# Queries and keys cast and turned inside the DMA, with key blocks of 96: one change to a fused attention and Fourier kernel

## The chip, the cores and the metric

The kernel runs on one core of a Trainium2 chip. The metric is the device time of one execution in microseconds (us), on the slowest core; here there is only one. Each kernel was run several times on the same chip as the kernel it is compared with. A run counts as slow when it lies more than 1.5% above the fastest of the same kernel. Ratios below use fast runs alone; medians are over all runs.

The engines are named as the profile names them: PE multiplies matrices, PEld loads its weights (beside PE), DVE is the vector engine, ACT the scalar engine, POOL is GpSimd, SP issues most of the loads. L344 is line 344 of the kernel that the trace belongs to. The same instruction has another line number in each version.

## The reference, cut to what matters

Attention in chunks of 32 queries; each chunk sees 8 memory rows and the keys from 16 before it to 8 after it. The result goes through a Fourier transform over sequence and features, a normalisation and a two-layer MLP.

```python
batch, n_heads, seq, head_dim, n_mem = 4, 8, 768, 64, 8
chunk, left_ctx, right_ctx = 32, 16, 8
for c in range(seq // chunk):
    k_full = concat([mem_k, k[c_start - 16 : c_end + 8]])      # clipped at the ends
    v_full = concat([mem_v, v[c_start - 16 : c_end + 8]])
    a = softmax(q_c @ k_full.T / sqrt(head_dim))
    out[c] = a @ v_full
x = out as (batch, seq, 512)
u = x + real(fft(fft(x, axis=1), axis=2))
result = u + relu(norm(u) @ w_ch1) @ w_ch2                      # 512 -> 2048 -> 512
```

## The kernel before

A "pair" is two heads. There are 16 pairs, four per batch, and a pair has 12 blocks of 64 queries. A plan written in the kernel gives every engine a fixed order of work before anything runs: an engine that has to wait does not take up later work. The cuts below keep the way of the keys, queries and values of one pair. Batch 0 is cast on DVE, later batches on POOL.

```python
RB = 8; QP = S // RB          # 96 partitions, each with 8 consecutive sequence rows
KP = QP + 8; NB = KP // 8; BS = 96; NT = S // 64

def e_load_q(n):              # 2 KB runs, fp32
    nc.sync.dma_start(qf[n % NS], q[b, 2*pr:2*pr+2].rearrange("h (p j) d -> p h (j d)", j=RB))
# ... e_load_k alike
def e_load_v(n, hh):          # values: own rows and memory rows; the rest is copied
    ...
def e_overlap(n, hh):
    nc.gpsimd.tensor_copy(v1[96:128, 0:NT, 0:D + 1], v1[0:32, 1:NB, 0:D + 1])

def e_cast_q(n, eng):         # eng: DVE in batch 0, POOL later
    eng.tensor_copy(qb_of[n].rearrange(cp_b), qf[n % NS].rearrange(cp_q, j=RB))
def e_turn_q(n):              # 8 transposes on PE, then ACT puts the rows into their natural order
    for j in range(RB):
        nc.tensor.transpose(trq[:, j*QP:(j+1)*QP], qb[:, j]..., ident_b[0:QP, 0:QP])
def e_qT(n):
    nc.scalar.copy(qT.rearrange("p (a j) -> p a j", j=RB), trq.rearrange("p (j a) -> p a j", j=RB))
# ... e_turn_k, e_kT alike; kTb holds key blocks at a pitch of 96, read 128 wide

def e_scores(n, g):
    for t6 in range(6):
        for hh in range(2):
            nc.tensor.matmul(sc[:, hh, t6, :], kT[r0:r0 + 64, t * BS:t * BS + P],
                             qT[r0:r0 + 64, ts(t, 64)], start=True, stop=True, ...)
...
t_w1 = [add("POOL", 0.7, lambda dt=dt: nc.gpsimd.dma_start(       # MLP weights, after batch 0
    w1_sb[:, dt, :], moe_w_ch1[ts(dt, P), :]), [x_last], moved=3.5) for dt in range(NDT)]
```

The softmax here doesn't subtract the row's maximum and nothing guards it: scores larger than these inputs give would overflow.

## Time and profile before

| | before |
|---|---|
| three runs, us | 341.11, 345.05, 346.55 |
| span of the profiled run, us | 339.3, granted clock 0.969 |
| PE busy, us | 289.6 |
| DVE, ACT, POOL busy, us | 183.2, 168.9, 80.6 |
| PE idle in the first 100 us | 28.6 |
| score matmuls (384), busy us | 12.8 |

Two more readings of before are needed for the comparison. First, two stretches of 20 us each. The columns are the stretch, its length, then busy us (and instructions) of PE, PE weight load, DVE, ACT, POOL, then granted clock, DMA share and GB/s.

```profile
40.00:60.00 20.00, 10.41 (x158) 8.54 (x158) 18.85 (x35) 15.18 (x24) 14.90 (x13) 0.98 1.12 205
60.00:80.00 20.00, 17.06 (x215) 13.96 (x216) 15.26 (x36) 10.39 (x18) 4.77 (x5) 0.85 1.14 196
```

PE works for 27 of these 40 us. (The DMA share sums the times of all packets over the 16 engines; it passes 1 where the recorded times of packets overlap.)

### The profile page before, as it was taken

How to read it: one execution, taken by the hardware profiler on the slowest of the kernel's cores; microseconds unless marked ns; L12 is line 12 of the kernel's file. 1: busy time of each engine (PE TensorE's matmuls, PEld its weight loads, DVE VectorE, ACT ScalarE, POOL GpSimd, SP SyncE). 2: the span in 40 equal slices, each digit the busy share in tenths (PEclk: the TensorE clock that was granted, in tenths of full speed). 3: DMA queues.
4: the chain of work that ended last, by engine and by line, in shares of the span. 5: the costliest groups of instructions: out<-in, count | busy, mean ns of one | idle time of the engine just before them, and what ended most of it. 6: DMA issues, size and time to landing. Idle time of an engine off the chain costs nothing.

```text
span 339.3 us, 6789 instructions
## 1 busy us (share of the span) xinstructions
PE 289.6 (85%) x2761; PEld 185.4 (55%) x2761; DVE 183.2 (54%) x356; ACT 168.9 (50%) x297; POOL 80.6 (24%) x89
## 2 busy tenths in 40 slices
PE   0678647969998886969999997898999999999995
PEld 0467536847565565547755654574445454554542
DVE  6964498868089899599773469782010100101001
ACT  7554885557637448676633623335436053250620
POOL 5634594224342637252001200000010000000000
PEclk9999999879999999898999999599999999999999
DMA  7999999999407785692063100000340100201001
GB/s 157 214 183 162 168 229 203 220 173 178 72 3 152 131 182 136 183 201 36 0 110 101 31 3 2 31 31 33 68 119 2 62 31 2 93 0 64 31 32 63
DMA packets 51839, 33.02 MB, mean 97 GB/s; under 512 B 40032, under 2 KB 42080, under 8 KB 51808
## 3 DMA queue, kind: packets, MB, share of 16 engines
q1 hardware_dynamic: 45376, 22.03, 36.9%
q0 software_dynamic: 2688, 4.19, 6.7%
q10 hardware_dynamic: 3744, 6.36, 4.9%
q8 instruction: 22, 0.36, 0.5%
q14 instruction: 9, 0.07, 0.1%
HBM read 28.11 MB, written 6.29 MB: 101 GB/s over the span
## 4 chain that ended last, share of the span: by engine, by line
PE 62%; DVE 14%; DMA 9%; ACT 4%; POOL 3%; issue 3%; SPq 3%; ACTq 0%; POOLq 0%
PE ph L496 23%; PE pc L510 22%; DMA qf<-in_q_dram 8%; PE xa L349 7%; PE pm L445 4%; PE ps L413 2%; SPq L261 2%; DVE zy L373 2%; DVE lo L403 2%; PE sc L325 1%; DVE ff L390 1%; DVE st L457 1%; DVE pq L381 1%; ACT e L333 1%; DVE pq L380 1%
## 5 line engine op out<-in xcount | busy, mean ns | idle before, releaser
L503 ACT ACTIVATE hT<-ph 128x384 f16<-128x384 f32 x128 | 61.2, 492 | 70.5 <-PE ph L496 70.3
L496 PE MATMUL ph<-unT,w_sb 128*128 128x384 f16 x512 | 92.2, 327 | 2.4 <-ACT hT L503 1.8
L510 PE MATMUL pc<-w_sb,hT 128*128 128x512 f16 x384 | 87.3, 382 | 0.0
L516 DVE SCALAR_TENSOR_TENSOR osb<-pc,rstd,xsb 128x512 f32<-128x512 f32 x24 | 17.8, 746 | 98.3 <-PE pc L510 98.3
L496 PEld LDWEIGHTS <-w_sb 128*128 128x128 f16 x512 | 48.3, 97 | 37.9 <-issue 8.2
L510 PEld LDWEIGHTS <-hT 128*128 128x128 f16 x384 | 37.2, 98 | 42.4 <-issue 1.5
L282 POOL COPY va<-va 32x780 f32<-32x780 f32 x32 | 36.2, 1138 | 50.0 <-DMA va<-in_v_dram 37.9
L333 ACT ACTIVATE e<-sc,mbias 128x384 f32<-128x384 f32 x64 | 33.7, 579 | 20.0 <-PE sc L325 19.1
L349 PE MATMUL xa<-va,e 128*64 128x65 f32 x768 | 35.4, 253 | 8.6 <-ACT e L333 3.7
L349 PEld LDWEIGHTS xa<-va,e 128*64 128x64 f32 x768 | 30.6, 162 | 15.7 <-issue 7.7
L463 ACT ACTIVATE un<-xsb,mu_s 128x512 f16<-128x512 f32 x24 | 17.3, 722 | 24.5 <-DVE mu_s L458 15.8
L359 DVE RECIPROCAL zs<-xa 128x6 f32<-128x6 f32 x32 | 6.1, 190 | 34.5 <-PE xa L349 34.3
L325 PE MATMUL sc<-qT,kTb 64*128 64x64 bf16 x384 | 12.8, 207 | 12.6 <-ACT kTb L314 11.0
L484 POOL TENSOR_SCALAR rstd<-mu_s 128x6 f32<-128x6 f32 x4 | 1.0, 244 | 89.7 <-DVE osb L516 83.7
L413 PE MATMUL ps<-cosS,lo 128*128 128x193 f16 (+1 forms) x72 | 16.6, 285 | 4.6 <-DVE lo L403 4.5
L274 POOL CAST qb<-qf 96x1024 bf16<-96x1024 f32 x12 | 14.9, 1242 | 20.8 <-DMA qf<-in_q_dram 11.9
L413 PE MATMUL ps<-cosS,hi 128*128 128x193 f16 (+1 forms) x72 | 16.7, 285 | 3.4 <-DVE ff L390 3.2
L425 ACT CAST up<-ps 128x386 f16<-128x386 f32 x16 | 9.7, 605 | 19.4 <-PE ps L413 17.8
L325 PEld LDWEIGHTS <-kTb 64*128 64x128 bf16 x384 | 8.8, 104 | 18.5 <-ACT kTb L314 12.3
L360 DVE TENSOR_TENSOR xsb<-xa,zs 128x384 f32<-128x384 f32 x32 | 17.8, 557 | 1.1
L398 ACT CAST hi<-ff 128x768 f16<-128x768 f32 x16 | 13.2, 832 | 10.1 <-DVE ff L390 9.9
L403 DVE TENSOR_TENSOR lo<-ff,hi 128x768 f16<-128x768 f32 x16 | 16.8, 1063 | 2.2 <-ACT hi L398 2.1
(90 smaller groups left out, 356.2 us busy)
## 6 DMA issues: line engine op xcount, KB each, us to landing
qf<-in_q_dram SPq DMA_DIRECT2D x16, 384.0 KB
kf<-in_k_dram SPq DMA_DIRECT2D x16, 384.0 KB
out_dram<-osb ACTq DMA_DIRECT2D x24, 256.0 KB, 2.0
va<-in_v_dram SPq DMA_DIRECT2D x32, 144.0 KB, 5.8
w_sb<-in_moe_w_ch_dram POOLq DMA_DIRECT2D x8, 512.0 KB, 16.1
va<-in_v_dram SPq DMA_DIRECT2D x32, 48.0 KB, 6.8
va<-in_mem_v_dram SPq DMA_DIRECT2D x32, 24.0 KB
unT<-un SPq DMA_TRANSPOSE x18, 2.4
```

Of the source, the lines that this page charges most:

```text
L282: nc.gpsimd.tensor_copy(v1[96:128, 0:NT, 0:D + 1], v1[0:32, 1:NB, 0:D + 1])
L325: nc.tensor.matmul(sc[:, hh, t6, :], kT[r0:r0 + 64, t * BS:t * BS + P], qT[r0:r0 + 64, ts(t, 64)], start=True, stop=True, tile_position=(r ...
L333: nc.scalar.activation(e1[:, :, :, ts(half, 32)], sc[:, :, 0:6, ts(half, 32)], AFT.Exp, bias=mbias[:, half:half + 1], scale=1.0 / math.sqr ...
L349: nc.tensor.matmul(xa[64 * half:64 * half + 64, st, hh, 0:65], e1[:, hh, t6, :], v1[:, 6 * g + t6, 0:65], start=True, stop=True)
L360: nc.vector.tensor_tensor(xs[b][:, 3 * g:3 * g + 3, 2 * pr * D:(2 * pr + 2) * D] .rearrange("p s (h d) -> p s h d", h=2), xa[:, :, :, 0:D] ...
L403: nc.vector.tensor_tensor(lo[:, ab].rearrange(fl), ff_of[b, par][:, ab].rearrange(fl), hi[:, ab].rearrange(fl), ALU.subtract)
L413: nc.tensor.matmul(out_[:, sp, :], part[:, ab, sp * 3 + st, c0:c1], tab[:, sp, st, :], start=(st == 0 and i == 0), stop=(st == 2 and i == 1))
L463: nc.scalar.activation(un, xs[b][:, kt, :], AFT.Identity, bias=mu_of[b][:, kt, 0:1], scale=-1.0)
L496: nc.tensor.matmul(ph[:, 0:384], w1_sb[:, dt, ts(ht, P)], unT_of[b][:, dt, sh * 384:(sh + 1) * 384], start=(dt == 0), stop=(dt == NDT - 1))
L503: nc.scalar.activation(hT_of[b, sh][:, ht, :], ph_of.pop((b, sh, ht))[:, 0:384], AFT.Relu, bias=0.0, scale=-1.0)
L510: nc.tensor.matmul(pc_of[b, sh, stl], hT_of[b, sh][:, ht, ts(stl, P)], w2_sb[:, ht, :], start=(ht == 0), stop=(ht == NHT - 1))
L516: nc.vector.scalar_tensor_tensor(osb, pc_of.pop((b, sh, stl)), rstd_of[b][:, st:st + 1], xs[b][:, st, :], ALU.mult, ALU.add)
```

## The change

Its intent: key blocks become exactly the 96 rows that a block of 64 queries can see (8 memory, 16 left, 64 own, 8 right), filled by DMA alone, so that POOL copies nothing. From batch 1 on, queries and keys are cast to bf16 by the DMA and turned by DMA transposes. PE, POOL and ACT are then rid of casts, transposes and copies. The core of the diff:

```diff
+OWN = NMEM + LEFT
+WIN = OWN + 64 + RIGHT                                   # 96
-    va = [spool.tile([P, NB, 66], FP32, ...) for i in range(6)]
+    va = [spool.tile([WIN, 2, NT, 66], FP32, ...) for i in range(3)]
-    kTb = [spool.tile([P, NB * BS], BF16, ...) ...]
+    kTb = [spool.tile([P, NT, WIN], BF16, ...) ...]
...
+    def e_load_qk(n, i):                                  # batches 1 to 3: fp32 to bf16 on the way
+        for hh in range(2):
+            nc.gpsimd.dma_start(dst[n % NS][0:QP, :, hh, :],
+                                src[b, 2 * pr + hh].rearrange("(p j) d -> p j d", j=RB))
+    def e_flip_q(n):
+        qT_of[n] = qT = apool.tile([P, RB, QP], BF16, tag="qT", bufs=2, name="qT")
+        nc.sync.dma_start_transpose(qT, qb[n % NS].rearrange("p j h d -> p (j h d)"))
+    def e_flip_k(n):
+        nc.sync.dma_start_transpose(kU[n % NKU][:, :, KR:KR + QP], kb[n % NS][0:QP]...)
...
-    def e_overlap(n, hh):                                 # and the clears, casts, PE turns of batches 1-3
-        nc.gpsimd.tensor_copy(v1[96:128, 0:NT, 0:D + 1], v1[0:32, 1:NB, 0:D + 1])
...
     def e_kT(n):
         nc.scalar.copy(
+            strided(kTb[n % NKT], NMEM, [[WIN, NT], [RB, 11], [1, RB]]),
+            strided(tr_of.pop((n, 1)), 0, [[64 // RB, NT], [1, 11], [KP, RB]])
+            if n < HP else
+            strided(kU[n % NKU], KR - KOFF, [[64 // RB, NT], [1, 11], [KS, RB]]))
     def e_scores(n, g):
-                nc.tensor.matmul(sc[:, hh, t6, :], kT[r0:r0 + 64, t * BS:t * BS + P],
-                                 qT[r0:r0 + 64, ts(t, 64)], ...
+                nc.tensor.matmul(sc[0:WIN, hh, t6, :], kT[r0:r0 + 64, t, :],
+                                 strided(qT[r0:r0 + 64], t * 64 // RB, [[1, 64 // RB], [QP, RB]]), ...
...
+            lq, lk = [add("POOL", 1.6, lambda i=i: e_load_qk(n, i),
+                          [t_cast[HP - 1]], take=(("qb", "kb")[i],), moved=1.8) for i in range(2)]
+            eq = add("SP", 0.1, lambda: e_flip_q(n), [lq, t_eq[0]], take=("qT",), ...)
+            tk = add("SP", 0.1, lambda: e_flip_k(n), [lk, t_uz[n % NKU]], take=("kU",), ...)
```

The turned queries lie as 8 groups of 96, so that 64 consecutive queries are read with a step of 96 elements. And `[t_cast[HP - 1]]`, by which the casts are to come after batch 0's last cast, is a condition in the plan's model.

## The prediction

> **What bounds the kernel now.** I read the page's slices first, then the chain that ended last in order of time, then four stretches of engine busy time, then the DMA view in narrow windows.
>
> From the page, busy tenths in 40 slices of 8.5 us:
>
> ```profile
> PE   0678647969998886969999997898999999999995
> ...
> DVE  6964498868089899599773469782010100101001
> ...
> POOL 5634594224342637252001200000010000000000
> ...
> DMA  7999999999407785692063100000340100201001
> ```
>
> The first ten slices are filled by DMA, not by PE; from slice 24 on PE is full and all else is nearly idle. The cuts below are mine: end of batch 0's attention (33 us), end of batch 1's (95), end of the last attention group (199), from the chain. Columns: stretch, its length, then busy us (and instructions) of PE, PE weight load, DVE, ACT, POOL, then granted clock, DMA share, GB/s.
>
> ```profile
> 0.00:33.00 33.00, 18.05 (x277) 15.20 (x279) 22.93 (x70) 19.64 (x28) 16.10 (x26) 1.00 1.07 181
> 33.00:95.00 62.00, 48.34 (x642) 36.77 (x638) 40.80 (x85) 40.74 (x68) 30.65 (x31) 0.94 0.99 172
> 95.00:199.00 104.00, 92.34 (x1135) 62.72 (x1132) 79.48 (x137) 59.80 (x107) 32.29 (x32) 0.97 0.51 104
> 199.00:340.00 141.00, 130.89 (x720) 70.69 (x718) 39.97 (x65) 48.74 (x95) 1.59 (x2) 0.97 0.12 40
> ```
>
> PE idles 14.9, 13.7 and 11.7 us in the first three, 40 us before the last attention ends. The DMA share is 1.0 for 95 us, then a half. The chain says what those 95 us wait for:
>
> ```profile
> 32.79 7.19 DMA qf<-in_q_dram
> ...
> 48.45 7.04 SPq L261
> ...
> 57.05 14.37 DMA qf<-in_q_dram
> 71.54 1.04 POOL qb L274
> ```
>
> So up to 72 us the input transfers carry the chain, with a POOL cast behind them. After 199 us there are only the MLPs and one Fourier stage, in PE's fixed order, ending at 339. **Two clocks** run: T, when the last attention group is through, and 140 us behind it.
>
> **What the Trainium skill says.** "DMA: Bandwidth & Descriptors", Specifications, asks for at least 512 B per transfer for line rate. The trace agrees. Two windows of 1 us, one of values (256 B runs), one of queries and keys (2 KB runs):
>
> ```profile
> DMA packets 527, 0.13 MB, mean 127 GB/s; under 512 B 527, under 2 KB 527, under 8 KB 527
> ...
> q1 hardware_dynamic: 527, 0.13, 142.2%
> ```
> ```profile
> DMA packets 113, 0.22 MB, mean 221 GB/s; under 512 B 5, under 2 KB 5, under 8 KB 113
> ```
>
> The same page, "SWDGE vs HWDGE vs iDMA": a cast during DMA can only be issued by GpSimd, the plain transpose only by the other queues. The change is built so; the casting queue here is the one of the weights. "SBUF — State Buffer" says that a VectorE operation with two SBUF inputs and a GpSimd operation that reads SBUF block each other. The trace agrees: POOL's value copy takes 827 to 4297 ns, and the DVE fold pq takes 1.27 us at 97 us, 0.83 at 209 when POOL is still. "TensorE: Matmul & The Clock Gate", Weight-path perf modes: fast weight load needs 128 weights not in fp32. Key blocks of 96 columns lose that in the score matmuls; no weight load of that kind is in this trace.
>
> **The change, part by part.** A pair is two heads; there are 16, four per batch.
>
> *PE.* Batches 1 to 3 lose 12 x 16 transposes. A group of 8 takes 0.37 to 0.39 us on the warm clock in the chain, so 24 x 0.38 = 9.1 us go, all from before T. The order of the changed kernel also moves MLP work: behind the last attention group stand 80 first-layer blocks and 65 second-layer blocks of four matmuls, against 81 and 72. With 0.65 and 0.86 us per block the tail sheds 0.65 + 6.0 = 6.7 us, which PE does before T instead. Score matmuls stay 384; their moving operand now steps 96 elements and the weights are 96 columns. A group of 12 takes 0.45 us; I allow 0.2 us more, 32 x 0.2 = 6.4 us, a guess. The value matmuls keep their column counts, hence their time.
>
> *POOL.* 32 value copies (36.2 us), 24 casts (14.9 + 13.0 us) and three large clears leave: 64 of its 81 busy us. It gets 48 casting DMAs to issue (a weight DMA takes 0.62 to 0.80 us of POOL, so an estimate of 40 us in sum, with nothing else to do). Copies stood between a landed value and its matmul, 0.83 us at least.
>
> *ACT.* 12 query copies (0.80 us) go, seven clears at the start too (4.3 + 2.1 us). The key copy grows from 832 to 1056 columns. ACT was at half load: worth little except in the first 10 us.
>
> *DVE.* Same work, but no POOL copies beside it. The 16 double pq and ff folds average 1.09 and 0.94 us against 0.85 undisturbed: 16 x (0.24 + 0.09) = 5 us, on the chain in the Fourier stages only; I count 3.
>
> *DMA.* Packets are counted by runs (the weights' queue shows it: 512 + 2048 runs + 8 x 16 completions = its 2688 packets). Before, a pair is 1728 value packets and 384 of 2 KB: 1728/527 + 384/113 = 3.3 + 3.4 = 6.7 us of all engines. Ten pairs and the weights (6.7% of the span, 23 us) make 90 us, and the DMA row goes quiet at 88: the sum holds.
> After, values are 2256 packets, since left, right and memory rows are fetched twice. A cast of q and k makes 4 x 768 = 3072 runs of 256 B read and 128 B written. Two transposes move 768 packets each; the transposes of this trace (2128 packets, 63.1% of 6 us) cost 28.5 ns of an engine, so 768 x 28.5/16 = 1.4 us each. How fast small packets go is the question. Saturated they came at 527 per us; the last two value loads alone took 18.6 ns each (1808 packets, 30.1% of 7 us), 860 per us. With the first rate a later pair costs 4.3 + 5.8 + 2.7 = 12.8 us, with the second 2.6 + 3.6 + 2.7 = 8.9 us. **I take 10.8**, against 6.7.
>
> **Sum.** T if DMA sets it: batch 0 until 33 us as now (four pairs at 4.3 + 3.4 = 31, plus the start), then 12 x 10.8 = 130, weights 23, twelve flips of the normalised rows at 0.95 us = 11, outputs and latencies 6: T = 203. T if PE's order sets it with its present idle: 198.9 - 9.1 + 6.7 = 196.5, less 3 (DVE), plus up to 6.4 (scores): 194 to 200. So the DMA bound lies slightly ahead. The tail is 140.4 - 6.7 = 133.7. 203 + 133.7 = 337 us of span, 2 to 3 below before. Where the rate is nearer 860 the span is 328 to 334. Before's runs lie 2 to 6 us above the profiled span; measured like the 345.05 median, and with the better rate somewhat likelier since neither POOL copies nor 2 KB queues stand in between, I say **336 us**.
>
> **Rivals.** (1) *PE bound with hidden transfers.* The DMA share of 0.51 from 95 to 199 us speaks for spare room, and POOL can issue loads far ahead; then transposes, copies and DVE blocking are saved and idle falls as well: span 322 to 330. Against it: three buffers per kind limit the lead. (2) *DMA becomes the bound.* Per pair it doubles at the slow rate; read-modify-write on 128 B could make casts slower than 256 B copies. At 12.8 us per pair T = 227 and the time is about 362. For it: 95 us already saturated. Against: MLP(0) is moved ahead of the waiting attention in PE's order, so there is filler. (3) *A head-of-line wait on SP.* Transposes wait for casts and stand in the same in-order queue as value loads; a late cast then delays later values too. It adds 5 to 15 us. (4) *Scores slow PE* by more than my 0.2 us per group: twice the present 0.45 us would add 14 us.
>
> **Range and chances.** 321 (rival 1, some idle gone) to 360 (rival 2). The faster line is near 338, just above my number, so faster over 2%: 0.48; within 2%: 0.28; slower: 0.24.
>
> **What would show it.** Casting queue: some 37,000 more packets, and their cost per packet (18 to 30 ns of an engine supports me; 45 refutes). PE transposes of the first batch alone. Score groups of 0.45 to 0.65 us. The end of the last value matmul near 200 us, and 134 us behind it. POOL busy under 25 us without issues. pq folds of 0.85 to 0.95 us. I am wrong if PE waits for qT, kTb or va grow past 15 us in the middle, or if score groups take 0.9 us.

## More of the kernel before

Second, the groups by line and form: line, engine, operation, output and inputs, shapes, count, then busy us and mean ns, and last the idle time before the group with what ended it.

```profile
L314 ACT COPY kTb<-trk 128x832 bf16<-128x832 bf16 x16 | 13.7, 854 | 5.6 <-PE trk L304 4.6 <-POOL va L282 0.9
...
L325 PE MATMUL sc<-qT,kTb 64*128 64x64 bf16 x384 | 12.8, 207 | 12.6 <-ACT kTb L314 11.0 <-ACT e L333 1.5
```

The copy of the turned keys into their blocks takes 854 ns on ACT, and the score matmuls read weights of 128 key columns.

## The result, and the profile after

The changed kernel takes 361.03 us (median of four, 358.30 to 361.70), the kernel before, measured with it, 344.03 (median of four, 341.11 to 346.55). The ratio is 1.051, with a 95% interval of 1.041 to 1.061. A ratio here is the mean time of one kernel's fast runs over the mean of the other's fast runs in the same rounds, so it is not quite the ratio of the medians. The change makes the kernel slower by 5%. The prediction of 336 us was wrong in direction, and the result lies just outside the range.

The spans agree with the times: 339.3 before, 356.6 after. The granted clock is no part of it (0.969 before, 0.979 after). The page of after, in tenths of 40 slices of 8.9 us, then its DMA queues with packets, MB and the share of the 16 engines' span:

```profile
PE   0672740057998999999968999989999999999995
...
DVE  7922334048880227888476885497740010201001
...
POOL 4071700330032422313300001000001000000000
...
DMA  4999999999309989969997242010160010100101
...
q1 hardware_dynamic: 68032, 19.48, 34.8%
q0 software_dynamic: 40320, 8.92, 29.4%
```

PE has a hole in slices 7 and 8 (about 53 to 71 us) that the kernel before does not have. PE's busy total hardly differs (290.6 against 289.6 us), and neither does DVE's or ACT's for the worse. So the time is waiting, and early. In numbers, by my own cuts: up to 100 us PE idles 53.3 us instead of 28.6. The last attention group ends at 229.5 us instead of 198.9, so that clock is 30.6 us late: PE idles 19.9 us more up to there (60.2 against 40.3) and works 10.7 us more. The part behind it takes 127.1 us instead of 140.4, 13.3 us less. The difference, 17.3 us, is that of the spans.

The same two stretches as before, now of after:

```profile
40.00:60.00 20.00, 7.57 (x117) 6.37 (x114) 9.19 (x25) 8.67 (x14) 2.98 (x4) 1.00 1.24 176
60.00:80.00 20.00, 5.06 (x60) 4.37 (x61) 3.50 (x4) 8.61 (x9) 5.97 (x8) 1.00 1.49 177
```

PE works 12.6 of the 40 us, and no other engine is busy for half of them, but the DMA share stays above 1. The chain that ended last, in order of time (start, us, what), names what is awaited:

```profile
49.56 4.39 SPq L281
...
54.06 15.35 DMA kU<-kb
...
69.49 6.86 DMA kU<-kb
...
76.43 0.88 ACT kTb L331
```

L281 is the transpose of pair 4's queries, `kU<-kb` that of pair 4's keys and then of pair 5's. From 50 to 76 us the chain is nothing but DMA transposes of the first two pairs of batch 1. The prediction had 1.4 us for each; here they take 15.4 and 6.9 us from issue to landing. The waits show how that reaches PE (us in all, times, longest us):

```profile
PE sc L344 <- ACT kTb L331: 21.5, 2, 20.3
DVE lo L422 <- ACT hi L417: 21.4, 6, 14.3
```

ACT stands before the key copy until the transpose has landed. Being in order, it holds the Fourier cast `hi` behind it, hence DVE, and PE stands before pair 4's scores with everything that comes later in its order.

The busy times of two groups have changed too:

```profile
L344 PE MATMUL sc<-qT,kTb 64*96 64x64 bf16 x384 | 27.3, 286 | 22.8 <-ACT kTb L331 21.5 <-ACT e L352 1.1 <-DMA qT<-qb 0.2
...
L331 ACT COPY kTb<-kU 128x1056 bf16<-128x1056 bf16 x12 | 24.1, 2028 | 19.1 <-DMA kU<-kb 17.9 <-DVE osb L535 1.2
...
L331 ACT COPY kTb<-trk 128x1056 bf16<-128x1056 bf16 x4 | 4.1, 1036 | 2.9 <-PE trk L321 2.9
```

The score matmuls cost 14.5 us more PE time than before, and one key copy of the later batches takes 2.03 us instead of 0.85. The last line is the same copy in batch 0, of the same size: it reads the turned keys from PSUM, in steps of 100 elements, and takes 1.04 us.

### The profile page after: what moved, and what is told of

Read it like the earlier page. It is cut to its first block, busy times and chain, and to the rows that moved or that the text cites. A ratio compares the mean times of both kernels' runs of the same rounds, so it can differ in the third digit from the quotient of the medians.

```text
span 356.6 us, 6371 instructions
## 1 busy us (share of the span) xinstructions
PE 290.6 (82%) x2569; PEld 183.8 (52%) x2569; DVE 171.8 (48%) x344; ACT 168.0 (47%) x278; POOL 52.7 (15%) x89
## 3 DMA queue, kind: packets, MB, share of 16 engines
q1 hardware_dynamic: 68032, 19.48, 34.8%
q0 software_dynamic: 40320, 8.92, 29.4%
## 4 chain that ended last, share of the span: by engine, by line
PE 66%; DVE 13%; DMA 11%; ACT 4%; SPq 3%; issue 2%; POOL 0%; ACTq 0%
PE pc L529 22%; PE ph L515 20%; PE xa L368 7%; DMA kU<-kb 6%; PE ps L432 6%; PE sc L344 5%; PE pm L464 5%; DMA lead<-in_k_dram 3%; DVE ff L409 2%; DMA va<-in_v_dram 2%; ACT e L352 2%; DVE zy L392 2%; SPq L293 1%; DVE lo L422 1%; SPq L281 1%
## 5 line engine op out<-in xcount | busy, mean ns | idle before, releaser
L515 PEld LDWEIGHTS <-w_sb 128*128 128x128 f16 x512 | 48.8, 97 | 41.5 <-issue 12.1
L352 ACT ACTIVATE e<-sc,mbias 96x384 f32<-96x384 f32 x64 | 33.4, 571 | 34.0 <-PE sc L344 25.8
L344 PE MATMUL sc<-qT,kTb 64*96 64x64 bf16 x384 | 27.3, 286 | 22.8 <-ACT kTb L331 21.5
L368 PE MATMUL xa<-va,e 96*64 96x65 f32 x768 | 35.9, 255 | 9.3 <-ACT e L352 6.5
L368 PEld LDWEIGHTS xa<-va,e 96*64 96x64 f32 x768 | 31.1, 165 | 18.9 <-issue 9.8
L344 PEld LDWEIGHTS <-kTb 64*96 64x96 bf16 x384 | 19.7, 145 | 28.6 <-ACT kTb L331 21.9
L331 ACT COPY kTb<-kU 128x1056 bf16<-128x1056 bf16 x12 | 24.1, 2028 | 19.1 <-DMA kU<-kb 17.9
L276 POOL DMA_DIRECT2D qb<-in_q_dram x24 | 18.8, 787 | 54.0 <-DMA qT<-qb 35.1
L482 ACT ACTIVATE un<-xsb,mu_s 128x512 f16<-128x512 f32 x24 | 17.3, 720 | 15.0 <-DVE mu_s L477 11.4
L276 POOL DMA_DIRECT2D kb<-in_k_dram x24 | 18.7, 781 | 35.7 <-DMA kU<-kb 34.4
L379 DVE TENSOR_TENSOR xsb<-xa,zs 128x384 f32<-128x384 f32 x32 | 17.8, 557 | 1.1
L470 DVE TENSOR_TENSOR xsb<-pm,xsb 128x512 f32<-128x512 f32 x24 | 16.1, 672 | 3.8 <-PE pm L464 3.6
L476 DVE BATCH_NORM_STATS2 st<-xsb 128x6 f32<-128x512 f32 x24 | 16.7, 694 | 0.8
## 6 DMA issues: line engine op xcount, KB each, us to landing
w_sb<-in_moe_w_ch_dram POOLq DMA_DIRECT2D x8, 512.0 KB, 17.4
```

Of the source, the lines that this page charges most:

```text
L276: nc.gpsimd.dma_start(dst[n % NS][0:QP, :, hh, :], src[b, 2 * pr + hh].rearrange("(p j) d -> p j d", j=RB))
L331: nc.scalar.copy(strided(kTb[n % NKT], NMEM, [[WIN, NT], [RB, 11], [1, RB]]), strided(tr_of.pop((n, 1)), 0, [[64 // RB, NT], [1, 11], [KP, ...
L344: nc.tensor.matmul(sc[0:WIN, hh, t6, :], kT[r0:r0 + 64, t, :], strided(qT[r0:r0 + 64], t * 64 // RB, [[1, 64 // RB], [QP, RB]]), start=Tru ...
L352: nc.scalar.activation(e1[:, :, :, ts(half, 32)], sc[0:WIN, :, 0:6, ts(half, 32)], AFT.Exp, bias=mbias[0:WIN, half:half + 1], scale=1.0 / ...
L368: nc.tensor.matmul(xa[64 * half:64 * half + 64, st, hh, 0:65], e1[:, hh, t6, :], v1[:, hh, 6 * g + t6, 0:65], start=True, stop=True)
L515: nc.tensor.matmul(ph[:, 0:384], w1_sb[:, dt, ts(ht, P)], unT_of[b][:, dt, sh * 384:(sh + 1) * 384], start=(dt == 0), stop=(dt == NDT - 1))
```

## The two theories

**Theory A, order and packets.** The eight weight loads (4.2 MB as written, not needed yet) are issued by POOL from 37 to 45 us, just ahead of pair 4's transposes. SP's view of the DMA queue shows the two transposes being issued (start, us):

```profile
45.30 8.65 SPq L281 DMA_TRANSPOSE qT<-qb  x1
54.06 5.62 SPq L284 DMA_TRANSPOSE kU<-kb  x1
```

The Trainium skill, "DMA: Bandwidth & Descriptors", Queues, rings and completion order, says that each DMA engine "round-robins between the queue rows it has work for, at *packet* granularity". If that holds here, the transposes, in packets of 256 B, move at the packet rate of the weights, however small they are. Three windows of 1 us of after (packets, MB, share). At 44 us, first-layer weights of 4 KB written per packet on q0:

```profile
q0 software_dynamic: 49, 0.19, 96.0%
q1 hardware_dynamic: 48, 0.01, 9.5%
```

At 62 us, second-layer weights of 1 KB per packet on q0:

```profile
q0 software_dynamic: 163, 0.15, 90.7%
q1 hardware_dynamic: 161, 0.04, 30.4%
```

At 69 us, as the weights end:

```profile
q1 hardware_dynamic: 683, 0.17, 102.7%
q0 software_dynamic: 122, 0.04, 36.0%
```

One packet of one queue for one of the other, at both sizes. (At 44 us the packets of q1 are still values; at 47 us, with the query transpose issued, the counts are 51 and 51.) When the other queue empties, q1 goes from 161 to 683 a microsecond. Theory A says: hold the weights back until the first two transposes have landed, and most of the loss goes.

**Theory B, a stepped operand.** The moving operand of the score matmuls steps by 96 bf16 elements, the source of the key copy by 128. The Trainium skill, "SBUF — State Buffer", in its note on cachelines, says that SBUF has 16-byte lines, that an access which goes to a new line pays, and that 8 bf16 elements lie within one. The traces of before and after agree in direction (12.8 and 27.3 us), but the number of weight columns changed with the step. Theory B says: make these rows contiguous, and score groups and key copies become short again. The rival within it: it is the 96-column weights that cost.

**Rivals to both.** The early casts delay batch 0 (the load of pair 3's keys is waited for 9.82 us in the chain); the new values by DMA, with rows fetched more than once, cost more than the copies they save; or the sheer number of packets is the bound, as the prediction's second rival had it. Each has a run below.

## The experiments

Medians of the kernel before in the three calls were 341.62, 342.87 and 342.22 us. Ratios are to it, in brackets the 95% interval. after was not measured again: its row is from its own call, in which the kernel before had 344.03.

| run | median us | ratio to before |
|---|---|---|
| after | 361.03 | 1.051 (1.041 to 1.061) |
| gate_casts | 361.01 | 1.057 (1.047 to 1.067) |
| gate_w | 341.35 | 1.001 (0.991 to 1.010) |
| gate_both | 339.86 | 0.998 (0.989 to 1.007) |
| natural | 351.33 | 1.032 (1.023 to 1.040) |
| wide | 359.38 | 1.055 (1.045 to 1.065) |
| blocks_only | 343.12 | 1.008 (0.997 to 1.019) |
| gates_natural | 332.18 | 0.973 (0.957 to 0.988) |
| all4 | 333.62 | 0.979 (0.971 to 0.988) |
| small_w | 365.48 | 1.075 (1.065 to 1.084) |
| before_gate | 342.84 | 1.010 (1.002 to 1.017) |
| natural_gate_w | 333.56 | 0.984 (0.977 to 0.992) |
| gates_natural_2 | 331.44 | 0.975 (0.967 to 0.983) |

So a difference to after depends on how it is taken. For gate_w it is 19.7 us by medians, 17 by ratios (5.0% of 342) and 14.6 by the spans of the profiled runs (356.6 and 342.0); for natural 9.7, 7 and 6.3. Where the text below gives one number, it is that of the medians.

### gate_w: the weights behind the transposes

From the changed kernel. A tiny POOL copy that reads pair 5's turned keys stands ahead of the first weight load. It is a real wait, on the landing of the transpose.

```diff
+    gate = cpool.tile([P, 2], BF16, name="gate")
+    def e_w1(dt):
+        if dt == 0:
+            nc.gpsimd.tensor_copy(gate[:, 1:2], kU[(HP + 1) % NKU][:, 0, KR:KR + 1])
+        nc.gpsimd.dma_start(w1_sb[:, dt, :], moe_w_ch1[ts(dt, P), :])
```

> The changed kernel with one small POOL copy ahead of the first weight load; it reads pair 5's turned keys, so that no weight load starts before the transposes of pairs 4 and 5 have landed. Order theory (on an engine a 256 B packet of a transpose takes turns with a 4 KB packet of the weights, 50 small packets per us instead of 700 or more): pair 4's key transpose lands at 55 us instead of 69, the 20.3 us wait of the score matmuls for kTb falls to 4 to 8, time 346 to 352. Volume theory: the weights come later, the first MLP matmuls wait for them instead, about 360.

Measured: 341.35 us, 15 to 20 us less than after and below the 346 expected. One line removes the loss against before. The transposes, from SP's view, and the second of the two stretches:

```profile
42.19 1.57 SPq L282 DMA_TRANSPOSE qT<-qb  x1
43.88 1.38 SPq L285 DMA_TRANSPOSE kU<-kb  x1
...
56.91 11.51 SPq L285 DMA_TRANSPOSE kU<-kb  x1
```

```profile
60.00:80.00 20.00, 17.13 (x174) 14.16 (x176) 13.05 (x26) 9.77 (x15) 3.88 (x5) 0.83 1.24 163
```

The query transpose is issued in 1.57 us instead of 8.65, the key transpose in 1.38 instead of 5.62. Pair 4's key copy starts at 54.9 us instead of 69.5, and PE is busy 17.1 of 20 us where it was 5.1. The weights are now issued from 54.2 to 59.3 us, 17 us later than in after, yet the MLP's first matmul comes at 87.0 us instead of 101.5: nothing on PE waits for weights in either trace. The slow issue has not gone: the third line is pair 6's key transpose, now beside the weights, over 11.51 us, but PE's wait for keys is down to 7.0 us in all. The order is shown as the cause. The packet counts above speak for turns by packet; the next run was to test that against bytes.

### small_w: the same weight bytes in smaller packets

From the changed kernel, without a gate. Each first-layer load is split by columns, so that its packets are read in 2 KB runs and written in 1 KB runs, four times as many.

```diff
+    def e_w1(dt):
+        for c in range(4):
+            nc.gpsimd.dma_start(w1_sb[:, dt, ts(c, DFF // 4)],
+                                moe_w_ch1[ts(dt, P), ts(c, DFF // 4)])
```

> The changed kernel, no gate; the first MLP weight matrix is loaded in 16 casting DMAs of 512 columns instead of 4 of 2048, so the same bytes go in packets of a quarter of the size (2048 of 2 KB read and 1 KB written, instead of 512). Turn-taking theory (an engine gives each queue one packet in turn, so the small packets beside the weights go at the weights' packet rate): pair 4's transposes, which got 50 packets per us beside the large packets, get about 150 as they do beside the second matrix; its keys land near 57 us instead of 69, the score matmuls' wait for kTb falls from 20 us to 6 to 10, time 348 to 354. Bytes theory (the transposes stand behind the bytes of the weights): they land at 69 as before, 359 to 362.

Measured: 365.48 us, some 4 us slower than after (8 by ratios). The chain of small_w:

```profile
47.36 14.13 DMA kU<-kb
...
66.94 15.91 DMA kU<-kb
```

The first part came as expected: pair 4's key copy starts at 61.6 us, 8 us earlier than in after, and PE's longest wait for it is 10 us instead of 20. In a window of 1 us at 47 us the weights' queue has 180 packets and the other 131, where beside the large packets they had 49 and 48. But the expectation for the time was a miss. The weights now run beside pair 5's transposes as well (168 and 137 packets at 69 us), which land at 82.9 us instead of 76.4, and that wait of 15.9 us gives everything back. Nor is the test clean: POOL issues the 16 loads from 39.3 to 56.2 us, as it waits for earlier ones in between, where after issues its 4 from 37.2 to 39.7. So fewer weight bytes lay ahead of pair 4's transposes, and their earlier landing fits the bytes theory too. The turns rest on the packet counts. What the run does show is that smaller packets alone do not put the transposes first; the gate does.

### gate_casts and gate_both: the early casts

In after, POOL issues the casts of pairs 4 and 5 from 17.8 to 26.0 us, while batch 0's loads are still coming. The gate makes POOL wait for DVE's cast of pair 3, as the plan had meant.

```diff
     def e_load_qk(n, i):
+        if n == HP and i == 0:
+            nc.gpsimd.tensor_copy(gate[0:QP, 0:1], kb[(HP - 1) % NS][0:QP, 0, 0, 0:1])
```

> The changed kernel with one small POOL copy ahead of the first casting load; it reads what VectorE casts for pair 3, so that no casting load starts before batch 0's own fp32 loads have landed (in the changed kernel the casting loads of pairs 4 and 5 are issued at 17.75 to 26 us, and pair 3's keys land only at 33.8). Order theory (small packets of later pairs share the engines with the loads that are needed now): the last value group of batch 0 starts near 41 us instead of 49.6, PE's wait before pair 4's scores may grow as its casts start later; in all 3 to 8 us less, about 354. Volume theory (all of it must pass the engines anyway): 360, within 1 per cent.

Measured: 361.01 us, as after; the 3 to 8 us expected did not come. The early part is won, though half of it: batch 0's eighth value group starts at 45.2 us instead of 49.6 (41 expected), and pair 4's key copy at 50.7 instead of 69.5. It is lost again at once, as the chain of this run shows:

```profile
44.91 13.73 DMA w_sb<-in_moe_w_ch_dram
...
58.73 16.22 DMA kU<-kb
```

Pair 5's transpose now stands beside the weights and lands at 75 us, as in after. The gain upstream of this untouched wait was worth nothing.

With both gates:

> Both gates, the same bytes and packets as the changed kernel. Order theory: the PE idle time in the first 100 us goes from 53 us back to about 33 (29 in the kernel before), time 340 to 347. Volume theory: 356 to 361, since nothing is taken off the engines.

Measured: 339.86 us, 1.5 us less than gate_w alone, with overlapping runs (338.33 to 342.11 against 340.22 to 343.69). Pair 5's key copy starts at 56.0 us, 20 us earlier than in after, and PE idles 35.0 us in the first 100 (33 expected). The early casts are a cause of the second order.

### natural: contiguous rows after the transpose

From the changed kernel. Only the mapping of sequence rows to partitions in the casting load is exchanged. Partition p gets rows p, p+96, p+192, ... instead of 8 consecutive ones. The casting loads write 64 elements per run in either case. After the transpose the rows are in natural order.

```diff
-                                src[b, 2 * pr + hh].rearrange("(p j) d -> p j d", j=RB))
+                                src[b, 2 * pr + hh].rearrange("(j p) d -> p j d", j=RB))
...
-                 strided(qT[r0:r0 + 64], t * 64 // RB, [[1, 64 // RB], [QP, RB]]), ...
+                 qT[r0:r0 + 64, ts(t, 64)], ...
...      # key copy of the later batches
-            strided(kU[n % NKU], KR - KOFF, [[64 // RB, NT], [1, 11], [KS, RB]]))
+            strided(kU[n % NKU], 0, [[64, NT], [1, WIN - NMEM]]))
```

> The changed kernel, queries and keys of batches 1 to 3 loaded with 96 consecutive rows over the partitions (same runs of 64 elements, same packets), so that the turned queries and keys lie in natural order: the moving operand of the scores has step 1, the key copy reads runs. Stride theory: a score group of 12 falls from 0.77 us to 0.45 to 0.5, key copies from 2.03 us to 1.1, PE work before the last attention group falls by 24 or more groups x 0.3 = 8 us, time 350 to 354. Weight-load theory (96 columns lose the fast load): the group stays at 0.7 or more, time 357 to 360.

Measured: 351.33 us, 6 to 10 us less than after. The groups of natural:

```profile
L347 PE MATMUL sc<-qT,kTb 64*96 64x64 bf16 x384 | 17.6, 233 | 25.3 <-ACT kTb L337 20.2 <-ACT e L355 2.1 <-DMA qT<-qb 1.8
...
L337 ACT COPY kTb<-kU 128x1056 bf16<-128x1056 bf16 x12 | 12.6, 1068 | 23.9 <-DMA kU<-kb 22.7 <-DVE osb L538 1.2
```

Score matmuls fall from 27.3 to 17.6 us, the 12 key copies from 24.1 to 12.6. The wait of 20.2 us for pair 4's keys stays, so this is gained apart from cause A. How much of it is PE's and how much ACT's shortened copy was not separated: both were undone together.

### wide and all4: 128-column weights

The rival within theory B. The key blocks are read 128 wide again, into rows of the result that nobody uses.

```diff
-                nc.tensor.matmul(sc[0:WIN, hh, t6, :], kT[r0:r0 + 64, t, :],
+                nc.tensor.matmul(sc[:, hh, t6, :], kTw[n % NKT][r0:r0 + 64, t * WIN:t * WIN + P],
```

> The changed kernel with one thing altered: score weights are read 128 columns wide (the block's 96 and the first 32 of the next, the scores of these rows are not used). The moving operand stays stepped by 96 elements. Weight-load theory: the score matmuls' busy time falls from 27.3 us by the 4.8 us that stand between the run with natural order (17.6) and the kernel before (12.8), to about 22, time 355 to 358. Stride theory alone: the stepped operand hides it, 27 us and 360, no change.

Measured: 359.38 us, no clear difference from after (1.055 against 1.051). The score group of wide:

```profile
L346 PE MATMUL sc<-qT,kTb 64*128 64x64 bf16 x384 | 26.3, 281 | 23.7 <-ACT kTb L333 23.4 <-ACT e L354 0.3
```

I had expected 22 us for this row; it fell only from 27.3 to 26.3. With the stepped operand the weights' width is hidden. With both gates and natural rows as well (all4):

> Both gates, natural order and 128 wide score weights: score matmuls at 13 us busy as before the change; 2 to 4 us below the run without the wide weights, 327 to 331, if PE's order sets the end; equal to it if the transfers do.

```profile
L352 PE MATMUL sc<-qT,kTb 64*128 64x64 bf16 x384 | 13.0, 208 | 7.7 <-ACT kTb L342 5.0 <-DMA qT<-qb 1.6 <-ACT kTb L338 1.1
```

Here the width shows: 13.0 us, as in the kernel before, against 17.4 with 96 columns in the same version (gates_natural). But the time does not follow: 333.62 us against 332.18 of gates_natural, with overlapping runs. The expected 327 to 331 were missed. The chains tell why: in both runs a key transpose of over 10 us stands between 104 and 117 us and holds ACT. It lands at 115.0 us in gates_natural and at 116.9 in all4, so that PE's savings before it end in this wait; the last attention group ends at 204.4 us in both.

### blocks_only: the first half of the change alone

The kernel before with the 96-row blocks, values wholly by DMA, and no POOL copies or clears. Queries and keys are cast on DVE and POOL and turned on PE as before.

```diff
-    va = [spool.tile([P, NB, 66], FP32, name=f"va{i}") for i in range(NV)]
+    va = [spool.tile([WIN, 2, NT, 66], FP32, name=f"va{i}") for i in range(NV)]
-    def e_overlap(n, hh): ...
+    # load_v, masks, key copy and score matmul as in the changed kernel, but the operand qT as before
```

> The kernel before with the first half of the change alone: key blocks of 96 partitions with left, right and memory rows brought by DMA, no POOL copies, no clears; queries and keys still loaded in fp32, cast on POOL and turned on PE. More value packets (2256 for 1728), no small packets of casts. If the second half did the harm: 336 to 344, score matmuls at 17 to 18 us busy (96 columns, step 1), the wait for query loads behind the weights stays as in the kernel before. If the value packets behind the weights do it: above 350.

Measured: 343.12 us, 1.008 (0.997 to 1.019). Neutral in sum. The value loads with rows fetched twice are not the loss. What freeing POOL of its copies is worth by itself stays open, as the run also pays for slower scores.

```profile
L331 PE MATMUL sc<-qT,kTb 64*96 64x64 bf16 x384 | 17.4, 231 | 7.3 <-ACT kTb L320 5.2 <-ACT e L339 2.0
```

Its score matmuls take 17.4 us, as in natural: the 4.6 us over before belong to 96 columns, the rest of after's 27.3 to the step.

### gates_natural, natural_gate_w and gates_natural_2: both causes taken away

Both gates and natural rows, nothing else:

> Both gates and the natural order. If the two causes are independent, the savings add: 340 less 8 to 10, 330 to 333, the first version below the kernel before by more than 2 per cent. If the score groups' gain is swallowed by waits for the transfers (DMA is near 1.3 of its share from 100 to 160 us with both gates): 336 to 340.

Measured: 332.18 us, 0.973 (0.957 to 0.988). Repeated in five rounds on another chip:

> The best version once more with five rounds, to narrow its interval against the kernel before: 329 to 334, ratio 0.965 to 0.98.

Measured: 331.44 us (six runs, one of them slow, 328.78 to 334.46), 0.975 (0.967 to 0.983). Natural rows with the weight gate alone:

> Natural order and the gate ahead of the weights, no gate ahead of the casts. The gate ahead of the casts had done nothing alone and 1.5 us beside the other: 331 to 335, the same as with both gates within 1 per cent. If it matters more here, 336 to 340.

Measured: 333.56 us, 0.984 (0.977 to 0.992). So gates_natural beats both kernels: the kernel before by some 2.5%, with intervals that leave open whether by more than 2%, and after by 7 to 8%. The causes add within the noise. By medians, 361.0 - 341.4 = 19.7 us for the order and 361.0 - 351.3 = 9.7 for the step make 29.4, and both together gave 361.0 - 331.4 = 29.6. So close an agreement is chance: by ratios it is 5.0% and 1.9% against 7.6%, by profiled spans 14.6 and 6.3 us against 25.0. The casts' gate, some 2 us by medians, is in the last figure of each.

### before_gate: is the order a fault of the kernel before too?

The kernel before with its weights behind pair 6's key load:

```diff
+            nc.gpsimd.tensor_copy(gate[0:KP, 1:2], kf[(HP + 2) % NS][:, 0, 0:1])
```

> The kernel before with a gate of the same kind: no weight load starts before pair 6's key load has landed (one POOL copy of a column). Its own chain waits 14.4 us for a query load at 57 to 71 us, beside the weights. If the cost of the weights' place in the order is a matter of the kernel before too: 332 to 338. If its 2 KB packets suffer little from it, or the MLP then waits for its weights: 341 to 345, and the gate pays only for the small packets of the change.

Measured: 342.84 us, 1.010 (1.002 to 1.017). No gain, if anything a small loss. This does not show that the weights do no harm in the kernel before. Its wait of 14.4 us for a query load is gone from the chain of before_gate. But the gate stands on POOL, which in this kernel also casts the keys: POOL waits 8 us at the gate, and pair 4's keys are cast at 57.5 us instead of 46.4. Gain and cost may cancel. In the kernel before, too, the queues take turns (46 packets of q0 and 49 of q1 at 50 us), with some of q1's packets of 2 KB. That the order hurts only the small packets of the change fits the result, but is not shown; a gate that leaves POOL free was not tried. What is shown is that this way of holding the weights back pays in the changed kernel and not in the kernel before.

## Why the prediction was wrong

**The step that failed first: the weights as one term in a sum of DMA time.** The prediction put "weights 23" and transposes of 1.4 us each into that sum and arrived at T = 203 us for the last attention group, measured 229.5. A sum of busy time does not ask who goes first. The weights moved in turns with the first transposes, and two key transposes took 15.4 and 6.9 us to land, in front of the two pairs for which PE, ACT and DVE had nothing else in their order. The filler that the prediction counted on against its second rival, MLP(0), was not there: PE stood idle for 20.3 us, and the first MLP matmul came at 101.5 us. gate_w shows 15 to 20 us for the order. The prediction's own sign of being wrong came true: the waits of the scores for `kTb` grew to 21.5 us, past its 15.

**The second: score groups and key copies.** The prediction allowed 6.4 us for the scores, called a guess, and nothing for a longer key copy than 832 to 1056 columns would make it. Measured: 14.5 us more of PE, and 14.5 us more of ACT for the key copies (24.1 + 4.1 against 13.7), of which only 16 x 0.18 = 2.9 go to the greater width (1.04 us in blocks_only against 0.85). natural gets 6 to 10 us back in time. The fourth rival had the right shape and called twice the group's time 14 us. It was weighed too lightly; the stepped operand was seen in the diff, and its cost was assumed.

**The rivals.** The third (a head-of-line wait on SP, 5 to 15 us) was nearest in kind. SP's queue did play its part: pair 5's casts had been issued by 26 us, but its key transpose only at 69.5, behind pair 4's slow transposes and values; in gate_w it was issued at 48.8. The cause it named, late casts, was wrong; the weights were the cause. From SP the wait passed on to ACT's key copy and PE's scores. The second named about 362 us, close to the result, for a reason that does not hold. If the number of packets were the bound, gates_natural, which moves the same 68,032 and 40,320, could not take 331 us. The first (transfers hidden, a span of 322 to 330) is nearly what gates_natural reaches, with a span of 331.6, though its chain still holds a key transpose of 10.7 us.

**What was right.** The casting queue has 40,320 - 2,688 = 37,632 more packets, as counted. The cost of a cast packet comes out as (29.4% x 356.6 x 16 - 364) / 37,632 = 35 ns of an engine, an estimate in which 364 us are the weights' share before (6.7% x 339.3 x 16); it lies between the 18 to 30 that were to support the prediction and the 45 that was to refute it. The recorded times of packets overlap, so this is what a packet took in this crowd, not what it costs alone. PE lost 192 transposes, 13.8 us of busy time (20.5 to 6.7) where 9.1 were expected. POOL fell from 80.6 to 52.7 us, 37.5 of them the 48 cast issues (40 estimated). DVE fell from 183.2 to 171.8 us without POOL's copies beside it. The part behind T lost more than the 6.7 us expected, 13.3: 7.3 us of second-layer matmuls (260 instead of 288, as read off the order), some 2 of Fourier rows at shorter means, and 3.6 us less idle. These gains are real in after too, but they lie behind a clock that ran 30.6 us late. With the two causes gone, the last attention group ends at 204.4 us in gates_natural. That is near the predicted 203, though not by the predicted sum, so it proves little of it.

**Two readings of before were loose.** Its chain is input transfers from 33 to 72 us only; up to 33 us it is mostly work of PE, ACT and DVE. And ACT is not nearly idle from slice 24 on (48.7 of the last 141 us). No sum rests on either.

**What stays open.** From 55 to 60 us of after, the engines moved 83 to 124 GB/s, about half of the windows around it, with both queues at work and still in equal turns (80 and 78 packets in one window). small_w has such stretches at 50 us (66 GB/s) and at 75 us (38 GB/s), the latter inside the wait that undid its gain. No run explains them. How natural's gain divides between PE and ACT was not measured, nor whether the kernel before would gain from weights held back without stopping POOL.

## What to carry to other kernels

When two queues share the DMA engines, count packets and ask whose are small and urgent: a bulk load of large packets that nobody needs yet belongs behind them, by a wait that exists on the chip and not only in a plan. A sum of DMA time says whether work fits, not whether it comes in time; read what each engine's fixed order holds behind the first late transfer. And choose the mapping of rows to partitions so that the turned operand comes out contiguous; here the load kept its 40,320 packets and the kernel gained 6 to 10 us.

## What the Trainium skill lacked or had wrong

- "DMA: Bandwidth & Descriptors", Queues, rings and completion order: turns by packet agree with the trace (49 and 48 packets in a microsecond beside 4 KB packets, 163 and 161 beside 1 KB). It speaks of several descriptors to a packet; the rows of this trace count one per run and alternate one for one in these counts. The consequence is missing: a queue of 256 B packets then has a fraction of the bytes, and went to 683 packets a microsecond when the other queue ran out. Holding the large packets back was worth 15 to 20 us of 361.
- The same page, Rules for kernel authors: "A transpose next to ordinary DMAs needs nothing" is about the result, and holds for it (all runs were correct); it lacks a word on the time. The issue of one query transpose took 8.65 us beside the weights and 1.57 without them.
- The same page, Specifications: that transfers should be 512 B or more agrees, but there is no figure for a casting load of 256 B read and 128 B written. Here about 35 ns of an engine per packet (an estimate, worked out above).
- "SBUF — State Buffer", the note on cachelines: the direction agrees, without a figure for the moving operand of a matmul or for ACT. With a step of 96 or 128 bf16 elements, 384 score matmuls took 27.3 us against 17.6 contiguous, and a key copy 2.03 us against 1.07. The same key copy from PSUM in steps of 100 took 1.04.
- "TensorE: Matmul & The Clock Gate", Weight-path perf modes: that 96 weight columns lose the fast load agrees (145 ns for a weight load against 105 with 128 columns). What it is worth depends on the operand beside it: 4.4 us of 384 matmuls with a contiguous one, 1.0 with a stepped one, and no measurable time of the kernel.
